# Feed-forward products whose moving columns come in turn from the two halves of a token tile

## The chip, the cores and the metric

The kernel runs on one NeuronCore of one Trainium2 chip. The metric is the device time of one execution in microseconds; the median of three runs of the kernel before is 1185.71 us (1185.4 to 1186.14).

## What is computed

The reference takes x of 2 sequences x 3008 positions x 256 features, does a complex linear layer with a soft threshold in the Fourier domain along each sequence, and two feed-forward layers on the 6016 resulting tokens. Cut to what matters:

```python
X = np.fft.rfft(x, axis=1)
Yr = X.real @ w_r - X.imag @ w_i + b_r
Yi = X.real @ w_i + X.imag @ w_r + b_i
# soft threshold by 0.01 on both, then y = irfft(Yr + 1j * Yi)

h = y @ w_in                                   # 256 -> 2048
y = (h * clip(h + 3, 0, 6) / 6) @ w_out        # 2048 -> 256

g = y @ w_gate                                 # 256 -> 1536
y = (silu(g) * (y @ w_val)) @ w_out2           # 1536 -> 256
```

All of it is in float32. A feed-forward layer treats every token by itself, so the order in which tokens stand in a tile does not matter to it.

## The kernel before, in words

Features lie on the 128 partitions and tokens along the free dimension. A matmul holds a 128 x 128 piece of a weight matrix in the array (the stationary operand) and streams a tile of tokens through it, column by column (the moving operand); the result is a tile of 128 output features by the same tokens in one PSUM bank.

Each float32 factor is kept as a high part of type fp32r and a low part, the rest. A product is then three matmuls on the same bank: low weights by high tokens, high weights by high tokens, high weights by low tokens.

The 6016 tokens are worked in pairs of blocks. `pairs` has six entries: five of 2 x 512 tokens and one of 2 x 448. `halves[s]` is the number of tokens of one block, 512 or 448, and it is the number of columns of nearly every feed-forward matmul.

The stages are these, all issued on TensorE in an order written out by hand (`seq`, then `quad1`, then `quad`):

- The Fourier part (`pre`, `s2`, `ln`, `ia`), up to 110 us and, with the first feed-forward units between its steps, up to some 195 us. `pre` uses plain float32 matmuls (L328, L330) of 512 columns, `ln` fp32r matmuls of 256 columns (L440 to L442).
- Layer one, first pair: `project1` multiplies a block by a piece of the first weights, `out1` multiplies the gated result by a piece of the second weights. Both call the helper `mm3` (L126 to L129), which issues the three matmuls.
- Layer one, other pairs: `quad1` takes two pieces of output features and two blocks at once, in seven products instead of eight, on sums and differences of weights and of tokens. The seven products go through `multiply(...)`'s inner function `product` (its three matmuls are L933, L934, L935) into the banks P, Tb and Q. The output again goes through `out1` and `mm3`. There are 40 such quads.
- Layer two: `quad`, 72 of them, again seven products by `product`; its output is summed by `share`, which calls `mm3`.

Between layers the token tiles go through SBUF or the DRAM tensor `Xd`. The results are written to `out_t` as features by tokens, and the host, after the run, turns this into tokens by features.

VectorE and ScalarE take each bank, add, gate and split it into high and low parts; they work column by column in place. SyncE's queue loads the split weights (`slot`) from DRAM two quads ahead.

Of the kernel before, what the change touches and what calls it, by code (L numbers as in the profile page):

```python
# [20 lines left out]
SEQ, DIM, NB = 3008, 256, 2  # L21
# [64 lines left out]
def fourier_moe_kernel(ctx: ExitStack, tc: tile.TileContext, x, lin, bias, w1, w2, fwd1, inv2, fwd2,  # L86
                       inv1, out):
    nc = tc.nc
# [34 lines left out]
    psf = [any_bank]  # L123
    few = [False]

    def mm3(o, wh, wl, xh, xl, start, stop):  # L126
        nc.tensor.matmul(o, wl, xh, start=start, stop=False)  # L127
        nc.tensor.matmul(o, wh, xh, start=False, stop=False)  # L128
        nc.tensor.matmul(o, wh, xl, start=False, stop=stop)  # L129
# [131 lines left out]
    p = [psf[0]([128, 512], f"p0_{n}") for n in range(2)]  # L261
# [230 lines left out]
    def L(p):  # L492
        return [lambda h=h: ln(*ORDER[p], h) for h in range(2)]

    def A(p):
        return [lambda: ia(*ORDER[p])] if p >= 0 else []
# [6 lines left out]
    for p in range(len(ORDER)):  # L503
        l, a = L(p), A(p - 1)
# [84 lines left out]
    def project1(k, f, n):  # L589
        xh, xl = xs1[k]  # L590
        wh, wl = weights(f, 0)
        p = bank([128, BLK], "ph")
        for dh in range(2):
            w = (slice(None), slice(dh * 128, dh * 128 + 128))
            mm3(p[:, :n], wh[w], wl[w], xh[:, dh, :n], xl[:, dh, :n], dh == 0, dh == 1)
        r = xs_p.tile([128, 512], F32, tag="r", name="r", bufs=3)
        nc.scalar.activation(r[:, :n], p[:, :n], AF.Relu, bias=three)
        nc.vector.scalar_tensor_tensor(out=r[:, :n], in0=r[:, :n], scalar=6.0, in1=p[:, :n], op0=ALU.min, op1=ALU.mult)
        return r
# [23 lines left out]
    def out1(k, f, e, hi, lo, first, last, where, tag):  # L623

        n = ntok(k)
        if first:
            acc[k, e] = where([128, BLK], f"acc{e}")
        wh, wl = weights(f, 1)
        w = (slice(None), slice(e * 128, e * 128 + 128))
        mm3(acc[k, e][:, :n], wh[w], wl[w], hi[:, :n], lo[:, :n], first, last)  # L630
        if last:
            finish1(k, e, acc.pop((k, e)), *tag)
# [292 lines left out]
    def multiply(x, q, n):  # L925

        def product(o, m, start=False):
            i = (1, 2, 4, 5, 6, 7, 3).index(m)
            t = slot[q]
            wh, wl = t[:, i], t[:, 7 + i]  # L930
            o = o[:, :n]

            nc.tensor.matmul(o, wl, x[m][:, 0, :n], start=start, stop=False, skip_group_check=not start)  # L933
            nc.tensor.matmul(o, wh, x[m][:, 1, :n], start=False, stop=False, skip_group_check=not start)  # L934
            nc.tensor.matmul(o, wh, x[m][:, 0, :n], start=False, stop=True, skip_group_check=not start)  # L935

        return product

# [144 lines left out]
    def quad(q):  # L1083
# [6 lines left out]
        def share(t, e):  # L1090
            if before is None:
                drain(2)
                return
            (pb, fb), w, g = before
            if (pb, t, e) not in acc:
                acc[pb, t, e] = acc_of(t, e)([128, BLK], f"acc{t}{e}")
            nb = halves[pb]
            mm3(acc[pb, t, e][:, :nb], w[:, 14 + e], w[:, 16 + e], g[t][0][:, :nb], g[t][1][:, :nb], fb == 0, fb == KF2 - 1)
            at = pairs[pb][0] + t * nb
            if fb == KF2 - 1 and pb == len(pairs) - 1 and t and e:  # L1100
                a = acc.pop((pb, t, e))
                for o, c, copy, send in ((hring(), slice(0, nb // 2), nc.vector.tensor_copy, nc.sync),
                                         (cring(), slice(nb // 2, nb), nc.scalar.copy, nc.scalar)):
                    copy(o[:, c], a[:, c])
                    send.dma_start(out[e * 128 : e * 128 + 128, at + c.start : at + c.stop], o[:, c])
            elif fb == KF2 - 1:
                o = xs_p.tile([128, 512], F32, tag="r", name="osb", bufs=3)
                if e == 0:
                    nc.scalar.copy(o[:, :nb], acc.pop((pb, t, e))[:, :nb])
                else:  # L1110
                    nc.vector.tensor_copy(o[:, :nb], acc.pop((pb, t, e))[:, :nb])
                nc.sync.dma_start(out[e * 128 : e * 128 + 128, at : at + nb], o[:, :nb])
# [66 lines left out]
    for q in range(len(quads2) + 1):  # L1179
        if q < len(quads2) and quads2[q][1] == 0 and quads2[q][0] + 1 < len(pairs):  # L1180
            p = quads2[q][0] + 1
# [50 lines left out]
```

## Time and profile before

| | before |
|---|---|
| median of three runs | 1185.71 us |
| span of the profiled execution | 1184.7 us |
| TensorE (PE) busy | 1175.7 us, 99% |
| weight loads (PEld) busy | 979.3 us, 83% |
| VectorE (DVE) busy | 914.2 us, 77% |
| ScalarE (ACT) busy | 781.1 us, 66% |
| GpSimd (POOL) busy | 48.0 us, 4% |
| matmuls | 6576 |
| moved by DMA | 219.63 MB |

The span runs from the first to the last instruction of one profiled execution; the device time is a little longer, since there is something before and after it. Matmuls are pipelined: the next one starts before the one before it has ended, so the distance from start to start says what one costs, and its own duration does not. A weight load runs beside the matmul before it.

### The profile page before, as it was taken

Reading aid. Unit: us, or ns where it says so; the run is one execution under the profiler, and the core shown is the slowest. Engines: PE = TensorE matmul, PEld = TensorE weight load, DVE = VectorE, ACT = ScalarE, POOL = GpSimd, SP = SyncE. Lnnn points to the kernel's source line nnn. Section 1 sums busy time; section 2 is a strip of 40 time slices with the busy share of each in tenths; the row PEclk is TensorE's granted clock in tenths of the full one; section 3 lists DMA queues with packets and bytes.
Section 4 is the critical chain, followed back from the end, with each engine's and each line's share of the span. In section 5 each row is a group of like instructions: output and inputs, shape, how many; then the busy total and the mean of one; then the engine's idle time right before and its main releaser. Section 6 shows DMA issues by size and latency. Waiting matters only on the chain.

```text
span 1184.7 us, 17959 instructions
## 1 busy us (share of the span) xinstructions
PE 1175.7 (99%) x6576; PEld 979.3 (83%) x6576; DVE 914.2 (77%) x1629; ACT 781.1 (66%) x1432; POOL 48.0 (4%) x79
## 2 busy tenths in 40 slices
PE   9999999999999999999999999999999999999998
PEld 3798888888888888888899888888888888888997
DVE  5588986898989989899987666766766766766665
ACT  3577765687787777777777655655655655655554
POOL 4000004400000000000000000000000000000000
PEclk9999999999999999999999999999999999999999
DMA  8987534874472572643553544644644644644551
GB/s 310 338 261 231 169 92 150 290 235 151 132 269 97 182 243 102 205 164 132 207 193 124 188 154 156 228 154 156 227 156 159 230 158 158 227 160 160 206 190 71
DMA packets 70184, 219.63 MB, mean 185 GB/s; under 512 B 6688, under 2 KB 30272, under 8 KB 58368
## 3 DMA queue, kind: packets, MB, share of 16 engines
q1 hardware_dynamic: 67280, 208.76, 50.9%
q0 software_dynamic: 2496, 9.05, 2.0%
q8 instruction: 51, 0.84, 0.3%
q10 hardware_dynamic: 320, 0.69, 0.2%
q14 instruction: 37, 0.30, 0.1%
HBM read 172.07 MB, written 46.40 MB: 184 GB/s over the span
## 4 chain that ended last, share of the span: by engine, by line
PE 97%; DMA 1%; DVE 1%; ACT 0%; issue 0%; SPq 0%; ACTq 0%
PE acc L127 13%; PE acc L129 13%; PE acc L128 13%; PE P L933 8%; PE P L934 8%; PE P L935 8%; PE Tb L935 4%; PE Tb L933 4%; PE Tb L934 4%; PE Q L933 2%; PE Q L935 2%; PE Q L934 2%; PE p L470 2%; PE p L396 2%; PE p L441 1%; PE p L442 1%
## 5 line engine op out<-in xcount | busy, mean ns | idle before, releaser
L990 ACT COPY hold<-P 128x512 f32<-128x512 f32 (+1 forms) x224 | 128.8, 575 | 78.8 <-PE P L935 78.0
L613 ACT CAST gated<-r 128x512 fp32r<-128x512 f32 (+1 forms) x160 | 98.0, 613 | 64.9 <-DVE r L981 56.6
L132 DVE TENSOR_TENSOR gated<-s,gated 128x512 fp32r<-128x512 f32 (+1 forms) x144 | 97.3, 676 | 49.7 <-ACT gated L1117 49.7
L985 DVE TENSOR_TENSOR hold<-Q,hold 128x512 f32<-128x512 f32 (+1 forms) x112 | 76.1, 679 | 68.0 <-PE Q L935 56.8
L132 DVE TENSOR_TENSOR gated<-r,gated 128x512 fp32r<-128x512 f32 (+1 forms) x160 | 107.9, 674 | 21.5 <-ACT gated L613 18.2
L127 PE MATMUL acc<-gated,w_o 128*128 128x512 f32 (+1 forms) x320 | 123.9, 387 | 0.0
L128 PE MATMUL acc<-gated,w_o 128*128 128x512 f32 (+1 forms) x320 | 123.1, 385 | 0.0
L129 PE MATMUL acc<-gated,w_o 128*128 128x512 f32 (+1 forms) x320 | 123.0, 384 | 0.0
L129 PE MATMUL acc<-gated,slot 128*128 128x512 f32 (+1 forms) x288 | 111.1, 386 | 0.0
L127 PE MATMUL acc<-gated,slot 128*128 128x512 f32 (+1 forms) x288 | 111.0, 385 | 0.1
L128 PE MATMUL acc<-gated,slot 128*128 128x512 f32 (+1 forms) x288 | 110.9, 385 | 0.0
L985 DVE TENSOR_TENSOR hold<-P,hold 128x512 f32<-128x512 f32 (+1 forms) x112 | 75.8, 677 | 38.6 <-PE P L935 38.6
L1157 ACT ACTIVATE s<-hold 128x512 f32<-128x512 f32 (+1 forms) x72 | 44.9, 623 | 86.3 <-DVE hold L985 86.3
L985 DVE TENSOR_TENSOR hold<-Tb,hold 128x512 f32<-128x512 f32 (+1 forms) x112 | 76.0, 678 | 27.6 <-PE Tb L935 19.5
L977 ACT ACTIVATE r<-hold,consts 128x512 f32<-128x512 f32 (+1 forms) x120 | 85.7, 714 | 17.4 <-DVE hold L985 15.0
L933 PE MATMUL P<-xo,slot 128*128 128x512 f32 (+1 forms) x240 | 91.8, 382 | 0.1
L934 PE MATMUL P<-xo,slot 128*128 128x512 f32 (+1 forms) x240 | 91.5, 381 | 0.0
L935 PE MATMUL P<-xo,slot 128*128 128x512 f32 (+1 forms) x240 | 91.4, 381 | 0.0
L1117 ACT CAST gated<-s 128x512 fp32r<-128x512 f32 (+1 forms) x144 | 88.2, 612 | 1.2 <-DVE s L1172 1.2
L981 DVE SCALAR_TENSOR_TENSOR r<-r,hold 128x512 f32<-128x512 f32 (+1 forms) x120 | 80.9, 675 | 4.6 <-ACT r L977 3.6
L1162 ACT ACTIVATE s<-hold 128x512 f32<-128x512 f32 (+1 forms) x72 | 45.0, 625 | 50.8 <-DVE hold L985 50.8
L990 ACT COPY hold<-Tb 128x512 f32<-128x512 f32 (+1 forms) x112 | 64.8, 578 | 7.6
(190 smaller groups left out, 2854.9 us busy)
## 6 DMA issues: line engine op xcount, KB each, us to landing
slot<-Wd SPq DMA_DIRECT2D x72, 1152.0 KB
slot<-Sd SPq DMA_DIRECT2D x40, 896.0 KB
st<-in_w SPq DMA_DIRECT2D x68, 256.0 KB
Wd<-slot SPq DMA_DIRECT2D x12, 1152.0 KB
z<-Bd SPq DMA_DIRECT2D x12, 512.0 KB
Cd<-cs POOLq DMA_DIRECT2D x12, 512.0 KB, 2.9
Xd<-x SPq DMA_DIRECT2D x20, 256.0 KB
raw<-Xd SPq DMA_DIRECT2D x5, 1024.0 KB
```

Source lines behind the costliest of these rows:

```text
L127: nc.tensor.matmul(o, wl, xh, start=start, stop=False)
L128: nc.tensor.matmul(o, wh, xh, start=False, stop=False)
L129: nc.tensor.matmul(o, wh, xl, start=False, stop=stop)
L132: nc.vector.tensor_tensor(out=o, in0=full, in1=hi.bitcast(F32), op=ALU.subtract)
L613: nc.scalar.copy(hi[:, :n], g[:, :n])
L933: nc.tensor.matmul(o, wl, x[m][:, 0, :n], start=start, stop=False, skip_group_check=not start)
L934: nc.tensor.matmul(o, wh, x[m][:, 1, :n], start=False, stop=False, skip_group_check=not start)
L935: nc.tensor.matmul(o, wh, x[m][:, 0, :n], start=False, stop=True, skip_group_check=not start)
L977: nc.scalar.activation(r[:, :n], x[:, :n], AF.Relu, bias=three)
L985: nc.vector.tensor_tensor(out=h, in0=x[:, :n], in1=c, op=ALU.add)
L990: nc.scalar.copy(c, x[:, :n])
L1117: nc.scalar.copy(hi[:, :nb], t[:, :nb])
```

## The change

Two helpers are added. `woven` gives a tile's columns in another order: for n columns it yields 0, n/2, 1, n/2 + 1, and so on, in turn from the first and from the second half. `pairwise` gives the output's columns as n/2 pairs, which is their order in memory. Both only change the access pattern of a matmul; no data is moved.

```diff
+    def woven(t):
+        return t.rearrange("p (a b) -> p b a", a=2)
+
+    def pairwise(t):
+        return t.rearrange("p (b a) -> p b a", a=2)
+
     def mm3(o, wh, wl, xh, xl, start, stop):
+        o, xh, xl = pairwise(o), woven(xh), woven(xl)
         nc.tensor.matmul(o, wl, xh, start=start, stop=False)
...
-            o = o[:, :n]
-            nc.tensor.matmul(o, wl, x[m][:, 0, :n], start=start, stop=False, skip_group_check=not start)
...
+            o = pairwise(o[:, :n])
+            hi, lo = (woven(x[m][:, i, :n]) for i in range(2))
+            nc.tensor.matmul(o, wl, hi, start=start, stop=False, skip_group_check=not start)
+            nc.tensor.matmul(o, wh, lo, start=False, stop=False, skip_group_check=not start)
+            nc.tensor.matmul(o, wh, hi, start=False, stop=True, skip_group_check=not start)
...
+    def unwoven(t):
+        return t.reshape(DIM, 2, -1, 2).swapaxes(2, 3).reshape(t.shape)
+
+    for _ in range(4):
+        parts = [unwoven(t) for t in parts]
```

So column 2b + a of a result holds the token that stood in column b of half a. A token tile passes four such products on its way, two in each layer, and the host undoes the four reorderings, within each block of a pair, when it lays out the result. The stationary operands, the tiles, the banks, the number and the order of the instructions, the semaphores and the DMAs are those of before.

## Rows read from the trace of the kernel before

**Rows 1.** The page, engines over the span, and PE in 40 slices.
```profile
span 1184.7 us, 17959 instructions
PE 1175.7 (99%) x6576; PEld 979.3 (83%) x6576; DVE 914.2 (77%) x1629; ACT 781.1 (66%) x1432; POOL 48.0 (4%) x79
...
PE   9999999999999999999999999999999999999998
```

**Rows 2.** The page, the chain that ended last, shares of the span by engine.
```profile
PE 97%; DMA 1%; DVE 1%; ACT 0%; issue 0%; SPq 0%; ACTq 0%
```

**Rows 3.** Busy time by stretch: length, engines (instructions), granted clock, DMA share, GB/s.
```profile
0.00:100.00 100.00, 95.26 (x577) 69.84 (x578) 66.39 (x136) 56.41 (x125) 18.39 (x33) 1.00 0.83 287
...
300.00:600.00 300.00, 300.00 (x1836) 250.19 (x1835) 271.46 (x504) 230.43 (x404) 0.00 (x0) 1.00 0.51 176
400.00:500.00 100.00, 100.00 (x693) 82.65 (x692) 91.04 (x172) 77.74 (x136) 0.00 (x0) 1.00 0.52 175
700.00:1100.00 400.00, 400.00 (x1768) 331.57 (x1767) 277.83 (x432) 237.97 (x415) 0.00 (x0) 1.00 0.50 180
```

**Rows 4.** Timeline of PE near 800 us (start, duration): first and last of 28.
```profile
799.83 0.39 PE L935 MATMUL P<-xo,slot 128*128 128x512 f32 x1
...
805.95 0.39 PE L935 MATMUL Tb<-xo,slot 128*128 128x512 f32 x1
```

**Rows 5.** Timeline of PE near 600 us: first and last of 32.
```profile
599.71 0.36 PE L935 MATMUL P<-xo,slot 128*128 128x448 f32 x1
...
605.99 0.36 PE L933 MATMUL P<-xo,slot 128*128 128x448 f32 x1
```

**Rows 6.** Timeline of PE near 70 us, Fourier part: first and last of 18.
```profile
69.95 0.28 PE L440 MATMUL p<-linl,X 128*128 128x256 f32 x1
...
71.99 0.28 PE L442 MATMUL p<-linh,X 128*128 128x256 f32 x1
```

**Rows 7.** Line 127 alone, then line 933 alone, over the whole span.
```profile
0.00:1185.00 1185.00, 286.10 (x736) 138.19 (x736) 1.00 0.53 185
0.00:1185.00 1185.00, 302.02 (x784) 147.19 (x784) 1.00 0.53 185
```

**Rows 8.** Groups by shape: the 448-column matmuls of lines 127 and 933.
```profile
L127 PE MATMUL acc<-gated,w_o 128*128 128x448 f32 x64 | 23.4, 365 | 0.0
L127 PE MATMUL acc<-gated,slot 128*128 128x448 f32 x48 | 17.6, 367 | 0.1
L933 PE MATMUL P<-xo,slot 128*128 128x448 f32 x80 | 29.3, 366 | 0.1
L933 PE MATMUL Tb<-xo,slot 128*128 128x448 f32 x40 | 14.6, 365 | 0.0
L933 PE MATMUL Q<-xo,slot 128*128 128x448 f32 x20 | 7.3, 366 | 0.0
```

**Rows 9.** Groups by shape: reads with and without a step, VectorE and ScalarE.
```profile
L179 DVE SCALAR_TENSOR_TENSOR wt<-st,wt 128x256 uint32<-128x256 uint32 x68 | 28.5, 419 | 0.1
L188 DVE SCALAR_TENSOR_TENSOR wt<-head,wt 128x256 uint32<-128x256 uint32 x32 | 13.4, 419 | 0.0
L170 ACT ACTIVATE head<-st 128x256 f32<-128x256 f32 x68 | 29.8, 439 | 0.0
L191 ACT CAST w_o<-wt 128x256 fp32r<-128x256 f32 x16 | 6.5, 409 | 2.2 <-DVE wt L188 2.2
```

**Rows 10.** The chain in order of time, first stage: start, time, what.
```profile
4.06 6.64 PE p L328 x8
10.69 12.03 PE p L330 x28
```

**Rows 11.** The chain in order of time, the end.
```profile
1175.50 0.64 DVE hold L985
...
1179.10 0.47 PE acc L127
...
1181.35 0.35 ACT hold L1104
```

More of the change, by code (lines that the diff above doesn't have):

```diff
@@ L930, in product @@
             wh, wl = t[:, i], t[:, 7 + i]
-            o = o[:, :n]
-            nc.tensor.matmul(o, wl, x[m][:, 0, :n], start=start, stop=False, skip_group_check=not start)
-            nc.tensor.matmul(o, wh, x[m][:, 1, :n], start=False, stop=False, skip_group_check=not start)
-            nc.tensor.matmul(o, wh, x[m][:, 0, :n], start=False, stop=True, skip_group_check=not start)
+            o = pairwise(o[:, :n])
[3 more added lines that the diff above has]
+            nc.tensor.matmul(o, wh, hi, start=False, stop=True, skip_group_check=not start)
         return product
```

## The prediction

> **What bounds the kernel now.** I read the page's table of engines first. TensorE (PE) is busy for 1175.7 of the 1184.7 us of the span, VectorE (DVE) for 77%, ScalarE (ACT) for 66%, and no slice of PE's line falls under 9 tenths but the last [rows 1]. A busy PE alone proves little, so the chain of waits comes next: 97% of the chain that ended last is PE, 1% DMA, 1% DVE [rows 2]. The stretches confirm it: from 300 to 600 and from 700 to 1100 us PE has no idle time at all, while DVE at its busiest (400 to 500 us) has 91 of 100 us and the DMA engines about half [rows 3]. So what an instruction of PE costs more is paid in full, and what the others do is hidden, and more so if PE gets slower.
>
> Then the pace of PE, which is not the duration of an instruction: durations are 389 ns, but the next one starts long before the end. In the timeline, 28 feed-forward matmuls of 512 columns start between 799.83 and 805.95 us: 6.12/27 = 226.7 ns apart [rows 4]. 32 of 448 columns start between 599.71 and 605.99 us: 6.28/31 = 202.6 ns [rows 5]. The 256-column ones of the Fourier part, of the same type, need (71.99 - 69.95)/17 = 120.0 ns [rows 6]. From 256 to 512 columns that is 106.7 ns for 256 columns, 0.417 ns each: one column per cycle at the 2.4 GHz that the granted clock of 1.00 stands for [rows 3]. What is left is fixed: 226.7 - 213.3 = 13.4 ns, at 256 columns 120.0 - 106.7 = 13.3 ns. The stream has no slack: columns enter at the array's full rate, and any delay in reading one lengthens the kernel.
>
> **How much of the time the change touches.** The lines of mm3 hold 736 matmuls each and those of the product 784 each [rows 7], on three lines each: 3 x (736 + 784) = 4560. Of 448 columns are 64 + 48 and 80 + 40 + 20 per line [rows 8], so 3 x 252 = 756; the other 3804 have 512. At the paces above they are 3804 x 226.7 + 756 x 202.6 ns = 862.4 + 153.2 = 1015.6 us. The other 169 us are the Fourier part, the inverse products and the two ends, where nothing is edited.
>
> **The change, part by part.**
>
> *Instructions.* None is added or removed: the same 4560 matmuls, in the same order, with the same weights and semaphores, on the same tiles and banks. SP's, ACT's and POOL's queues and every DMA stay. No wait is added. The price of this is 0, and PE itself is its cover.
>
> *The output* (pairwise). Taken as pairs one behind the other it is the same row of addresses in the same order as before: 0. What reads the banks (ACT, DVE) works on columns in place: 0. The host's four reorderings lie outside the time.
>
> *The moving operand* (woven). This is the whole edit. Two neighbouring columns now lie 256 tokens of 4 bytes apart (224 in the last pair), and every step jumps. No row shows a moving operand read so; in the trace every one is a contiguous row. So I bound it.
> From below: no extra time per column, 226.7 and 202.6 ns stay. A gain I exclude up to measurement: the columns already go in at one per cycle, and the fixed 13.4 ns is not in the reading of columns, since it is the same at 256 and 512. The nearest rows on that side are steps on other engines: DVE's L179 reads words 8 bytes apart in 419 ns, just as its contiguous L188 of the same form, and ACT's L170 reads the same words in 439 against 409 ns of L191 [rows 9]. But these engines take over 1 ns per column there, more than twice what a matmul has.
> From above: the plain fp32 matmuls of the first stage, where a column occupies PE for two cycles: 28 of L330 in 12.03 us, 430 ns for 512 columns [rows 10]. The far end are the eight of L328 before them, 6.64/8 = 830 ns [rows 10].
> I take two cycles per column. It is the next whole step above one at the full clock, it is a pace at which PE is seen to run, and a step per column cannot be hidden, since nothing else in the row waits. A stream that asks for a new place in each of 0.417 ns has more than doubled the demand of any row that I can see here.
> With the fixed part kept, since it did not move with the number of columns: 512 columns gain 512/2.4 = 213.3 ns, 448 gain 186.7 ns. 3804 x 213.3 + 756 x 186.7 = 811.4 + 141.1 = **952.5 us**. With L330's pace instead (430 - 226.7 = 203 ns, where the fixed part shrinks to 3 ns; 376 - 202.6 = 174 ns for 448) it is 772 + 132 = 904 us; if the fixed part doubles too, 952.5 + 3804 x 13.4 + 756 x 15.9 ns = 1016 us.
>
> What the trace says of this read is only that a contiguous one reaches one column per cycle [rows 4, 6]. [...]
>
> *What is late next.* While a 512-column matmul takes 440 instead of 227 ns, DVE's 91 of 100 us become some 47 of 100 (times 226.7/440), ACT's 78 some 40, and the DMA share halves [rows 3]; weights and operands come earlier by PE's clock than now, so no new wait arises. The end stays: from 1175.50 us on the chain runs through DVE and ACT to the last copy at 1181.35 us [rows 11], with five matmuls behind 1179.10 us that add about 5 x 0.19 = 1 us, counted in the sum already. The first 110 us hold no feed-forward product and stay.
>
> *The sum.* The profiled span is 1184.7 us, the median of the runs 1185.7, so 1.0 us lies around it. 1184.7 + 952.5 + 1.0 = **2138 us**. Own range 2089 (L330's pace) to 2201 (fixed part doubled).
>
> **Rivals.**
>
> *Not slower: the reader keeps up.* If PE's read fetches ahead or holds both halves open, it delivers a column per cycle wherever it lies. Place: the same 4560 matmuls; price 0; time 1185.7 us. It decides as long as a column costs no more than 0.417 ns. The margin is thin: 0.2% of the time, about what a measurement of this kernel can tell from no change, is 2.4 us, or 0.5 ns in a matmul. For it: two halves are only two running places, each of which is contiguous in itself, and DVE's stepped read is free [rows 9]. Against it: there PE's rate is more than twice the demand. The case that the change does nothing (the address order undone on the way to the chip) gives the same time; against that speaks that only the operand's order changes and the output's does not, so it cannot cancel. Together 0.28.
>
> *Partly hidden.* A reader that holds some of what it has opened pays for every second column: 1.5 cycles, half the sum, 1185.7 + 476 = 1662 us. For it: the neighbour of a column in its own half follows two columns later, so that what was opened for the one may still be at hand for the other. Against: no row shows any pace between one and two cycles per column. 0.11.
>
> [...]
>
> *Faster.* Only if reading in turn from two places took something off the fixed 13.4 ns; at L330's 3 ns that would be 4560 x 10 ns = 47 us, 1139 us. 0.02.
>
> **How the numbers follow.** Two cycles per column 0.55; not slower 0.28; partly hidden 0.11; worse 0.04; faster 0.02. Slower by over 0.2% is 0.55 + 0.11 + 0.04 = 0.70, within 0.2% 0.28, faster 0.02. The time is that of the likeliest case, 2138 us, with its own range of 2089 to 2201. The range that is to hold the time must take in the second case, which alone holds more than 2 in 10, so it runs from 1183 to 2201 us; it is in truth two places with little between them.
>
> **What the profile after would show.** If I am right: the starts of the 512-column matmuls of both lines are 430 to 455 ns apart and of the 448 ones 376 to 405, while the 256-column ones of the Fourier part stay at 120; the weight loads' share of the span falls from 83% to under 50%, DVE's to about 43%; the counts stay; the granted clock stays 1.00; and from 110 us on every stretch is longer by the same factor per matmul. [...]

## The result, and the profile after

The changed kernel takes 1139.44 us (median of 4 runs, 1138.95 to 1140.27), the one before 1185.57 us in the same comparison: a ratio of 0.961, 95% interval 0.960 to 0.963. Slower by 952 us was forecast; it is faster by 46 us.

The page of the changed kernel, engines over the span and the chain by engine (compare [rows 1, 2]):

```profile
span 1138.5 us, 18052 instructions
PE 1126.9 (99%) x6576; PEld 982.7 (86%) x6576; DVE 913.1 (80%) x1629; ACT 778.5 (68%) x1432; POOL 48.5 (4%) x79
...
PE 93%; DVE 3%; DMA 2%; ACT 1%; issue 1%; POOL 0%; SPq 0%; ACTq 0%; DVEq 0%; POOLq 0%
```

The same matmuls and the same work on DVE and ACT, and 48.8 us less of PE. The page counts 93 instructions more, 18052 for 17959 [rows 1]; by the trace PE's sequencer has 105 more semaphore instructions (184 for 79), VectorE's 12 fewer. They do not explain the gain: the kernel below whose two places lie 8 bytes apart also has 18052, and gains nothing. The stretches (columns as in [rows 3]) have the same granted clock of 1.00 as before, so the clock is not what changed. More matmuls fit into each: 1882 against 1768 from 700 to 1100 us.

```profile
300.00:600.00 300.00, 298.77 (x1901) 263.03 (x1900) 280.49 (x520) 238.93 (x423) 0.00 (x0) 1.00 0.54 183
400.00:500.00 100.00, 100.00 (x712) 86.59 (x711) 94.69 (x177) 81.25 (x143) 0.00 (x0) 1.00 0.57 191
700.00:1100.00 400.00, 400.00 (x1882) 355.01 (x1881) 289.19 (x456) 249.01 (x437) 0.00 (x0) 1.00 0.54 192
```

The pace tells where it went. The timeline of PE near 770 us, the first and the last of 29 matmuls of 512 columns (compare [rows 4]):

```profile
769.77 0.38 PE L943 MATMUL P<-xo,slot 128*128 128x512 f32 x1
...
775.82 0.38 PE L137 MATMUL acc<-gated,slot 128*128 128x512 f32 x1
```

6.05/28 = 216.1 ns, where it was 226.7. Near 575 us, the first and the last of 19 of 448 columns (compare [rows 5]): 3.40/18 = 188.9 ns, where it was 202.6.

```profile
574.95 0.35 PE L136 MATMUL acc<-gated,w_o 128*128 128x448 f32 x1
...
578.35 0.35 PE L136 MATMUL acc<-gated,w_o 128*128 128x448 f32 x1
```

From 256 to 512 columns the pace before grows by 226.7 - 120.0 = 106.7 ns [rows 4, 6], 0.417 ns per column; by that 512 columns are 213.3 ns and 448 are 186.7. After the change 448 and 512 columns are 216.1 - 188.9 = 27.2 ns apart, 0.425 ns per column, so the columns cost about what they did, and of the fixed 13.4 ns (15.9 at 448 columns) 2.8 and 2.2 are left. The 256-column matmuls of the Fourier part, which were not edited, keep theirs: 18 of them start between 69.40 and 71.44 us, 2.04/17 = 120.0 ns, as in [rows 6].

By these paces the change should have brought 3804 x 10.6 + 756 x 13.7 ns = 40.3 + 10.4 = 50.7 us; the span is 46.2 us shorter. The rest went into waits. Added up from the starts, the gaps between feed-forward matmuls (distances more than 40 ns over the pace) are 5.2 us before and 11.8 us after, most of the growth between 200 and 600 us. The waits of PE's weight loads for the results of VectorE and ScalarE in the seven products, before (first fence) and after (time, times, longest):

```profile
PEld P L933 <- DVE hold L985: 0.9, 2, 0.5
```

```profile
PEld P L943 <- DVE hold L995: 5.3, 11, 1.1
PEld P L943 <- ACT hold L1000: 2.0, 7, 0.6
```

### The profile page after: what moved, and what is told of

Read it like the earlier page. It is cut to its first block, busy times and chain, and to the rows that moved or that the text cites. A ratio compares the mean times of both kernels' runs of the same rounds, so it can differ in the third digit from the quotient of the medians.

```text
span 1138.5 us, 18052 instructions
## 1 busy us (share of the span) xinstructions
PE 1126.9 (99%) x6576; PEld 982.7 (86%) x6576; DVE 913.1 (80%) x1629; ACT 778.5 (68%) x1432; POOL 48.5 (4%) x79
## 4 chain that ended last, share of the span: by engine, by line
PE 93%; DVE 3%; DMA 2%; ACT 1%; issue 1%; POOL 0%; SPq 0%; ACTq 0%; DVEq 0%; POOLq 0%
PE acc L136 12%; PE acc L138 12%; PE acc L137 12%; PE P L943 8%; PE P L945 8%; PE P L944 8%; PE Tb L943 4%; PE Tb L944 4%; PE Tb L945 4%; PE Q L943 2%; PE Q L944 2%; PE Q L945 2%; PE p L479 2%; PE p L405 2%; PE p L450 1%; PE p L451 1%
## 5 line engine op out<-in xcount | busy, mean ns | idle before, releaser
L136 PE MATMUL acc<-gated,w_o 128*128 128x512 f32 (+1 forms) x320 | 120.4, 376 | 0.0
L137 PE MATMUL acc<-gated,w_o 128*128 128x512 f32 (+1 forms) x320 | 119.6, 374 | 0.0
L138 PE MATMUL acc<-gated,w_o 128*128 128x512 f32 (+1 forms) x320 | 119.6, 374 | 0.0
L138 PE MATMUL acc<-gated,slot 128*128 128x512 f32 (+1 forms) x288 | 108.1, 375 | 0.0
L136 PE MATMUL acc<-gated,slot 128*128 128x512 f32 (+1 forms) x288 | 108.0, 375 | 0.1
L137 PE MATMUL acc<-gated,slot 128*128 128x512 f32 (+1 forms) x288 | 107.9, 375 | 0.0
L943 PE MATMUL P<-xo,slot 128*128 128x512 f32 (+1 forms) x240 | 90.2, 376 | 1.5 <-DVE hold L995 1.4
L944 PE MATMUL P<-xo,slot 128*128 128x512 f32 (+1 forms) x240 | 88.8, 370 | 0.0
L945 PE MATMUL P<-xo,slot 128*128 128x512 f32 (+1 forms) x240 | 88.8, 370 | 0.0
L995 DVE TENSOR_TENSOR hold<-Tb,hold 128x512 f32<-128x512 f32 (+1 forms) x112 | 75.8, 677 | 14.2 <-PE Tb L945 10.4
L991 DVE SCALAR_TENSOR_TENSOR r<-r,hold 128x512 f32<-128x512 f32 (+1 forms) x120 | 80.9, 674 | 2.6 <-ACT r L987 1.5
```

Source lines behind the costliest of these rows:

```text
L943: nc.tensor.matmul(o, wl, hi, start=start, stop=False, skip_group_check=not start)
L944: nc.tensor.matmul(o, wh, lo, start=False, stop=False, skip_group_check=not start)
L945: nc.tensor.matmul(o, wh, hi, start=False, stop=True, skip_group_check=not start)
L995: nc.vector.tensor_tensor(out=h, in0=x[:, :n], in1=c, op=ALU.add)
```

## The experiments

Where nothing else is said, a time is that of one run; runs of the kernel before beside them took 1183.8 to 1187.4 us. The paces in the text after a list of rows are means over all pairs of neighbouring matmuls with the same number of columns in the trace, the lowest and the highest tenth left out.

**Only mm3 is woven.**

```diff
-            o = pairwise(o[:, :n])
-            hi, lo = (woven(x[m][:, i, :n]) for i in range(2))
+            o = o[:, :n]
+            hi, lo = (x[m][:, i, :n] for i in range(2))
...
```

> Only the helper mm3 reads in turn from the two halves (2208 matmuls); the 2352 of the seven products read their columns in a row, as before. If each woven matmul saves its own part of the fixed time (226.7 to 216.1 ns at 512 columns, 202.6 to 188.9 at 448), the 336 of mm3 with 448 columns and the 1872 with 512 save 4.6 + 19.8 = 24 us: about 1161 us, and the timeline shows two paces side by side. Theory 'place': the shorter distance is the one behind a woven matmul. Theory 'boundary' (the time is lost between two matmuls and depends on both): the first contiguous one behind a woven one, or the first woven one behind a contiguous one, has a pace of its own.

1166.11 us. PE's timeline, woven products (L136 to L138) and the contiguous ones behind them:

```profile
802.42 0.38 PE L136 MATMUL acc<-gated,slot 128*128 128x512 f32 x1
802.64 0.38 PE L137 MATMUL acc<-gated,slot 128*128 128x512 f32 x1
802.85 0.38 PE L138 MATMUL acc<-gated,slot 128*128 128x512 f32 x1
803.07 0.38 PE L136 MATMUL acc<-gated,slot 128*128 128x512 f32 x1
803.28 0.38 PE L137 MATMUL acc<-gated,slot 128*128 128x512 f32 x1
803.50 0.38 PE L138 MATMUL acc<-gated,slot 128*128 128x512 f32 x1
803.72 0.40 PE L943 MATMUL P<-xo,slot 128*128 128x512 f32 x1
803.95 0.39 PE L944 MATMUL P<-xo,slot 128*128 128x512 f32 x1
804.17 0.39 PE L945 MATMUL P<-xo,slot 128*128 128x512 f32 x1
804.40 0.39 PE L943 MATMUL P<-xo,slot 128*128 128x512 f32 x1
```

0.65/3 = 217 ns behind a woven matmul, 0.68/3 = 227 ns behind a contiguous one. At the borders the means of the whole trace are 216 ns from a woven to a contiguous one and 229 to 230 the other way. Each matmul saves its own time: 'place', not 'boundary'. The saving is 4 us short of the 24 expected; up to 600 us the contiguous ones are a little slower than before (means of 230 ns, later 228). Why, is open.

**Other orders of the columns.** The helpers `woven` and `pairwise` are replaced, and the host's layout with them; the rest is the changed kernel. First runs of two columns from each half (with c=4 in place of c=2 for runs of four), then all even columns before all odd ones:

```diff
-        return t.rearrange("p (a b) -> p b a", a=2)
+        return t.rearrange("p (a b c) -> p b a c", a=2, c=2)
```

> The two halves again, in turn, but two neighbouring columns (8 bytes) from each. Theory 'place' (the fixed part is lost where neighbouring columns lie next to each other, in the same small stretch of memory): some or all of the 10.6 ns come back, pace between 216 and 227 ns, 1139 to 1185 us. Theory 'form' (any moving operand with more than one dimension in its access pattern loses nothing): 216 ns, about 1139 us.

> As the run of twos, with four neighbouring columns (16 bytes) from each half. 'Place': pace nearer to 227 ns than with twos, 1160 to 1185 us. 'Form': 216 ns, about 1139 us.

```diff
-        return t.rearrange("p (a b) -> p b a", a=2)
+        return t.rearrange("p (b a) -> p a b", a=2)
```

> All even columns, then all odd ones: every column lies 8 bytes behind the one before it. 'Place' with a stretch of 16 bytes: two columns in each, so between 216 and 227 ns, or above 227 ns if a step costs something. 'Form': 216 ns, about 1139 us. If what helps is that neighbours are far apart (in another block of the memory), 227 ns and 1185 us.

1651.86, 1280.01 and 2183.84 us. All three have more than one dimension in their pattern and all are slower: 'form' is out. So is the simple 'place', by which runs of four should come near the contiguous pace and no further. PE's timelines, first and last of 14, of 18 and of 10 matmuls: 4.34/13 = 334, 4.26/17 = 251 and 4.06/9 = 451 ns.

```profile
1154.61 0.50 PE L944 MATMUL P<-xy,slot 128*128 128x512 f32 x1
...
1158.95 0.50 PE L138 MATMUL acc<-gated,slot 128*128 128x512 f32 x1
```

```profile
894.74 0.42 PE L136 MATMUL acc<-gated,slot 128*128 128x512 f32 x1
...
899.00 0.41 PE L945 MATMUL Q<-xy,slot 128*128 128x512 f32 x1
```

```profile
1526.50 0.63 PE L944 MATMUL Tb<-xy,slot 128*128 128x512 f32 x1
...
1530.56 0.63 PE L137 MATMUL acc<-gated,slot 128*128 128x512 f32 x1
```

Even then odd, at 451 ns, is close to the 440 that were forecast, for the most harmless-looking of the orders. That led to a count that orders the paces; it is a rule of thumb of mine, and how the columns are read no trace shows. Of every second column of the stream it asks how many follow each other within one aligned stretch of 16 bytes, four words. In a row they are 0, 2 | 4, 6: two, and 227 ns. In turn from two halves, 0, 1, 2, 3 of the first half: four, and 216 ns. Even then odd, 0 | 4 | 8: one, and 451 ns. The other two runs did not fit from the start: runs of four, 0, 2 | 256, 258 | 4, 6, count two as in a row, and yet a matmul takes 250 ns and not 227; runs of two, 0 | 256 | 2 | 258, count one as even then odd and take 334 ns.

**In turn from near places.** The two places lie four words apart, then two words (b=2):

```diff
-        return t.rearrange("p (a b) -> p b a", a=2)
+        return t.rearrange("p (k a b) -> p k b a", a=2, b=4)
```

> In turn from two places that lie only four words (16 bytes) apart: columns 0, 4, 1, 5, 2, 6, 3, 7, 8, 12, ... [...] Theory 'far apart' (the gain comes from neighbours in different halves, 1 KB apart): 227 ns or more, 1185 us or more. Theory 'jumps cost' (every jump of the pattern but the first form costs something, as the runs of two did): 250 to 333 ns, 1280 to 1650 us.

> In turn from two places two words (8 bytes) apart: 0, 2, 1, 3, 4, 6, 5, 7, ... [...] 'Far apart': 227 ns too. 'Jumps cost': 250 to 333 ns.

1140.33 and 1185.08 us; 'far apart' and 'jumps cost' are out. The timelines, 21 and 20 matmuls: 4.32/20 = 216 and 4.30/19 = 226 ns. By the count the first order has four (0, 1, 2, 3), as the two halves with 216 ns, and the second two (0, 1 | 4, 5), as columns in a row with 227.

```profile
796.62 0.38 PE L943 MATMUL P<-xy,slot 128*128 128x512 f32 x1
...
800.94 0.38 PE L138 MATMUL acc<-gated,slot 128*128 128x512 f32 x1
```

```profile
827.66 0.39 PE L945 MATMUL Q<-xy,slot 128*128 128x512 f32 x1
...
831.96 0.39 PE L136 MATMUL acc<-gated,slot 128*128 128x512 f32 x1
```

**The tile xo moved by two words,** in the kernel with places 16 bytes apart:

```diff
-    even = cv.tile([128, 7, 2, BLK], F32R, name="xo")
-    rooms = [[even[:, i] for i in range(7)]]
+    even = cv.tile([128, 7, 2, BLK + 4], F32R, name="xo")
+    rooms = [[even[:, i, :, 2 : 2 + BLK] for i in range(7)]]
```

> The kernel that reads in turn from two places 16 bytes apart, but the tile xo begins two words (8 bytes) later; the tiles xy, gs and gated stay where they are. [...]

1154.75 us. Groups by shape: the same product into the same bank from the moved tile and from two that stayed. The kernel before has the duration of 389 ns with its pace of 227, the changed kernel's pace of 216 goes with 379. By the starts, the products of the moved tile are 230 ns apart (203 at 448 columns), those of xy and gs 216.

```profile
L943 PE MATMUL Tb<-xo,slot 128*128 128x512 f32 x80 | 31.1, 389 | 0.0
L943 PE MATMUL Tb<-xy,slot 128*128 128x512 f32 x52 | 19.7, 379 | 0.0
L943 PE MATMUL Tb<-gs,slot 128*128 128x512 f32 x52 | 19.7, 379 | 0.0
```

So alignment matters: a tile that starts 8 bytes later loses the gain (230 ns), while its neighbours keep it (216). The count has this too: from word 2 on, columns 0, 1 | 2, 3 lie two and two in aligned 16 bytes, as in a row.

**Four quarters, eight parts.** `a=4` and `a=8` in place of `a=2` in both helpers.

> In turn from the four quarters of the tile: 0, 128, 256, 384, 1, ... [...] 'Far apart', or any theory by which a jump to another part of the tile is free: 216 ns, 1139 us.

> In turn from the eight eighths of a tile: 0, 64, 128, ..., 448, 1, ... [...]

1424.31 and 2312.02 us; 16 and 10 matmuls: 4.25/15 = 283 and 4.38/9 = 487 ns.

```profile
995.61 0.45 PE L945 MATMUL Q<-xy,slot 128*128 128x512 f32 x1
...
999.86 0.45 PE L945 MATMUL P<-xy,slot 128*128 128x512 f32 x1
```

```profile
1616.61 0.67 PE L138 MATMUL acc<-gated,slot 128*128 128x512 f32 x1
...
1620.99 0.67 PE L945 MATMUL Tb<-xy,slot 128*128 128x512 f32 x1
```

'Far apart' is out again: four quarters take 283 ns and not 216. Both orders count one (0 | 256 | 1 | 257 and 0 | 128 | 256 | 384), as even then odd with 451 ns; four quarters stay far below that, eight parts go above it. So the count gives neither; why four quarters cost 283 ns, and runs of two, which also count one, 334, is open. One explanation was not tested: that the price depends on how far apart the places lie. The last pair of blocks speaks for it. There they lie 224, 112 and 56 words apart in place of 256, 128 and 64, and runs of four, four quarters and eight parts cost 11, 35 and 181 ns more than a contiguous stream, where in proportion to the columns it would be 21, 50 and 228; even then odd, which steps by 8 bytes but for one jump, costs 193 where in proportion it would be 197.

**The weight loads.** Three runs on the kernel before ask whether the load beside a contiguous stream takes the fixed time. In the first, the loads of the first and second of three matmuls read otherwise; in the others, the second's load is shorter (64, then 96 columns).

```diff
-            nc.tensor.matmul(o, wl, x[m][:, 0, :n], ...
-            nc.tensor.matmul(o, wh, x[m][:, 1, :n], ...
+            ws = t[:, 6 + i : 8 + i].rearrange("p k c -> p (k c)")[:, ::2]
+            w0 = t[:, i, :1].to_broadcast([128, 128])
+            nc.tensor.matmul(o, ws, x[m][:, 0, :n], ...
+            nc.tensor.matmul(o, w0, x[m][:, 1, :n], ...
```

> The kernel before, moving columns in a row, but in the seven products the stationary operand is read otherwise: that of the first of three matmuls takes every second word of two pieces of weights, that of the second takes one word 128 times, the third is as before. (So the products are not those of the reference; only their pace is looked at.) A weight load runs beside the matmul before it. If the fixed 13.4 ns of a contiguous stream come from the weight load beside it, the first matmul's distance to the second (beside the load of a single word) falls to 216 to 220 ns, the second's to the third stays at 227 to 230, and the third's to the next first (beside the load with steps) rises by up to 10 ns. If the fixed part lies in the moving stream alone, all three stay at 227 to 230 ns.

```diff
-            nc.tensor.matmul(o, wh, x[m][:, 1, :n], start=False, stop=False, skip_group_check=not start)
+            nc.tensor.matmul(o[:64], wh[:, :64], x[m][:, 1, :n], start=False, stop=False, skip_group_check=True)
```

> The kernel before, moving columns in a row; of the three matmuls of each of the seven products the second (L934) has a stationary operand of 64 columns instead of 128 (so half of its features get no contribution from it). Its load is shorter (135 ns where the trace has a load of 64 columns) and runs beside the first matmul's stream. Theory 'the load steals' (the 10.6 ns are taken by the reads of the weight load that runs beside the stream): the distance from the first matmul to the second falls from 227 to some 221 ns, the others stay. Theory 'late start' (each matmul starts late by the same time and readers without slack never make it good): all stay at 227 to 230 ns.

> As the load of 64, with 96 columns in the second matmul's stationary operand. 'The load steals': first to second some 224 ns, so between 227 and what the load of 64 shows. 'Late start': 227 to 230 ns. If the load of 64 shows a distance of its own at the second matmul itself and this one does not, that belongs to the narrower array and not to the load.

1202.71, 1195.56 and 1201.04 us. In the first, the mean distances of the three are 233, 233 and 231 ns, beside the load of one word too. With the load of 64, the groups of loads (third number: mean ns of one) and a stretch of PE's timeline:

```profile
L933 PEld LDWEIGHTS P<-xo,slot 128*128 128x128 f32 x240 | 45.0, 188 | 9.6 <-DVE hold L985 0.8 <-ACT hold L990 0.6
L934 PEld LDWEIGHTS P<-xo,slot 128*64 128x64 f32 x240 | 32.2, 134 | 7.8
```

```profile
801.98 0.39 PE L933 MATMUL P<-xo,slot 128*128 128x512 f32 x1
802.20 0.40 PE L934 MATMUL P<-xo,slot 128*64 128x512 f32 x1
802.44 0.39 PE L935 MATMUL P<-xo,slot 128*128 128x512 f32 x1
802.67 0.39 PE L933 MATMUL P<-xo,slot 128*128 128x512 f32 x1
```

The load is 54 ns shorter and the distance beside it (L933 to L934) has a mean of 228 ns; with the load of 96 it is 232. Nothing falls to 221 or 224. All three kernels are slower as a whole, though, and 512-column matmuls that were not edited went to 226 to 232 ns (why, is open), so these distances alone do not settle it. The 448-column ones do better: with the load of 64 the other distances have means of 201 to 204 ns, about the 203 of before, and the distance beside the short load is 204. 'The load steals' is not borne out in this form.

**The Fourier part woven too** (three rounds), and **the weight sums on GpSimd** (three rounds), each on top of the change:

```diff
+            o = pairwise(o)
...
-                wh, wl = linh[:, k, dh], linl[:, k, dh]
+                wh, wl = woven(linh[:, k, dh]), woven(linl[:, k, dh])
...
```

> The changed kernel, and the 432 matmuls of 256 columns in the Fourier part read their moving columns in turn from two halves as well (the bias, the first weights' rows and nothing else are laid out accordingly by the host). Theory 'late start' (every matmul loses the same few ns at its start, whatever its length, and a stream whose readers have slack makes them good): 256 columns go from 120.0 to 109.4 ns, 432 x 10.6 ns = 4.6 us less at most, of which the waits of this part for VectorE, ScalarE and DMA may keep a part: 1135 to 1139 us. Theory 'spread' (the loss grows with the columns that are read): 256 columns would lose half of what 512 lose, but before the change both lost 13.4 ns, so it would have to stay at 120 or fall by 5: 1137 to 1139.5 us.

1137.28 us, ratio 0.960 (0.958 to 0.961) to the kernel before. 17 distances of the 256-column matmuls, (71.61 - 69.72)/17 = 111 ns where it was 120:

```profile
69.72 0.27 PE L450 MATMUL p<-linl,X 128*128 128x256 f32 x1
...
71.61 0.28 PE L452 MATMUL p<-linh,X 128*128 128x256 f32 x1
```

The gain is there also at 256 columns, which 'spread' does not give, but it is 8 to 9 ns (mean pace 111.6 for 119.7) and not the 10.6 of 'late start'. Some 5 ns stay over the 106.7 of the columns. The plain float32 matmuls of L405 in the same trace, 128 columns (L330 takes 0.84 ns for each, [rows 10]) and with the same 128 x 128 load beside them, also start 111.6 ns apart. That the load sets a floor there, which would keep the rest, is a guess from these two paces; no run tests it. The time fits both theories' ranges, so it is the pace that decides. The median is 2.2 us under that of the changed kernel (1139.44), and this is the fastest version run; the intervals of the two ratios overlap, so that it beats the change is likely rather than shown.

```diff
-                weight_sums(F)
+                weight_sums(F, nc.gpsimd)
...
```

> The changed kernel, with the 48 sums of second-layer weights on GpSimd instead of VectorE (and the copies behind them in another order, so that ScalarE does not wait). It asks whether what the change did not gain, some 4.6 us between the paces' 50.8 and the span's 46.2, is given back in waits of PE for VectorE in the first layer. Theory 'VectorE is late there': 13.7 us of VectorE's work go, of its 280 in 300 to 600 us, and the waits of PE on its line hold<-... shrink: 1135 to 1138 us. Rival (the waits come from bursts elsewhere, or ScalarE now waits for GpSimd): 1139 us or more.

1141.31 us, ratio 0.963 (0.961 to 0.964): nothing gained. PE's loads still wait for VectorE as long:

```profile
PEld P L943 <- DVE hold L995: 5.6, 13, 0.7
PEld P L943 <- ACT hold L1000: 2.8, 7, 0.7
```

VectorE's busy time from 300 to 600 us fell only from 280.5 to 276.8 us, since what was left on it took longer there: L991, for one, has a mean of 694 ns in place of 676 (its groups that read hold), L184 of 317 in place of 287. So the run did not take the work away as meant, and says little on 'VectorE is late there'. Where the 4.5 us are given back is shown by the waits; how to get them is not.

## Why the prediction was wrong

- *What bounds the kernel* was right: PE, at its own pace, and the split of 226.7 ns into 213.3 for columns and 13.4 fixed. What the traces show for it is 106.7 ns for 256 columns at a granted clock of 1.00, so 0.417 ns per column or 2.4 columns per ns, which is all that the prediction's 2.4 GHz rests on; twice the 106.7 ns are the 213.3. The counts of 3804 and 756 matmuls turned 10.6 and 13.7 ns into 50.7 us.
- *The moving operand* failed, at "I take two cycles per column". The step looked at the distance between one column and the next. The runs show that a jump at every column can be free: the change (216 ns) and two places 16 bytes apart (216) jump at each, and are faster than columns in a row (227). The count of every second column fits the change, the two places 16 and 8 bytes apart, the moved tile and even then odd; runs of two (334) and of four (250), four quarters (283) and eight parts (487) do not fit it. The pace that was forecast was real and one edit away (even then odd, 451 ns against the 440 forecast). By the paces measured, 952.5 us should have been -50.7. (L328's 830 ns were read from the chain; its starts are 853 ns apart. The forecast does not use them.)
- *The exclusion of a gain* failed too, and it is the costlier mistake: the fixed 13.4 ns "is not in the reading of columns, since it is the same at 256 and 512". The runs show that it is: the order of the columns alone takes it from 13.4 to 2.8 ns. That each stream starts late and only one with slack catches up would be such a loss; this is a guess, and no run shows a late start. [Rows 10] had a smaller fixed part in sight: L330's 430 ns are 3 ns more than twice the 213.3. I used the row only as a price for slowness. Nor was the fixed part the same everywhere: the prediction's own 202.6 ns leave 15.9 at 448 columns.
- *The rival 'faster'* was the right one, in size and place: "took something off the fixed 13.4 ns; at L330's 3 ns that would be 4560 x 10 ns = 47 us, 1139 us". It had a chance of 0.02, since nothing in the trace, as I read it, tied the fixed part to the order of reading; it gave no reason why the part should go. That its 1139 us meet the measured 1139.44 so closely is luck in part: 10 ns was too little (10.6 and 13.7), and 4.5 us of waits, which it did not have, made up for it.
- *Output, instructions, queues, the end of the chain* at 0 held (the semaphore instructions that came with the edit cost nothing that shows). *What is late next* was worked out for a slower PE only; with a faster one PE waits for VectorE's and ScalarE's results in the first layer, which took 4.5 of 50.7 us.

What stays open: why a contiguous fp32r stream loses 10.6 ns per matmul. A late start that is made good only with slack agrees with the paces at 256 and 512 columns and with L330, and roughly with the Fourier part woven; it does not say why 448 columns get 13.7 ns back and 512 get 10.6. The weight load as its taker was tested and not found; no run shows the start itself.

## What to carry to other kernels

Where PE is busy all the time, compare the distance of matmuls with 0.417 ns per column (the step here at a granted clock of 1.00), and ask of a fixed rest whether any row with a lighter stream is without it. For fp32r moving operands like these (no other type was woven), let every second column be the neighbour in memory and keep the tile aligned to 16 bytes: places 16 bytes apart in turn do as well as two halves (216 ns each, 230 in a tile that starts 8 bytes later), with no reordering beyond eight tokens. Avoid a step of two elements, runs of two or four, and four or more places in turn: they cost 10% to 115% per matmul here (250 to 487 ns for 227).

## What the runs showed of the hardware that was not expected

- Count every second column by itself: with two neighbours in each aligned 16 bytes (in a row; 0, 2, 1, 3) a 512-column fp32r matmul takes 227 ns, with four (two halves in turn; places 16 bytes apart) 216, with one (step of two) 451. The count does not cover orders that go back and forth between far places: runs of four have two and take 250 ns; runs of two, four quarters and eight parts have one and take 334, 283 and 487.
- The order of the moving columns alone spans 216 to 487 ns for the same 512-column matmul at the same granted clock of 1.00.
- Weight loads slow down with the stream beside them: means of 188 ns beside a contiguous one, 195 beside runs of two, 208 beside even then odd and beside eight parts.
